# Attention with a gated feed-forward on one core: pooled PSUM banks, product streams in halves, and V products of one or two key tiles in a list-scheduled order

## The chip, the cores and the metric

The kernel runs on one core of one Trainium2 chip. The metric is the device time in microseconds of one execution; a time is the median of the runs. A core has TensorE (PE in the profile) with its weight loads (PEld), VectorE (DVE), ScalarE (ACT), GpSimd (POOL) and SyncE (SP), whose queue issues the DMAs. Each engine works through its own instructions in their order, and semaphores hold an instruction until what it needs has been done.

## The reference

```python
xn = _layernorm(x)                                   # S = 2048, D = 512
q, k, v = split((xn @ wqkv), 32 heads of 16)
p = softmax(q @ k.T * 16 ** -0.5)                    # 2048 x 2048 for each head
s = concat(p @ v) @ wo
h = (xn @ w_gate) * (xn @ w_up)                      # F = 1792
y = h @ w_down
out = x + s * silu(y)
```

All is float32 to the caller. Inside, each operand of the projections and of the feed-forward is split into a high part (float32r) and the rest, and each product is made of three terms: high x high, high x low, low x high.

## The kernel before, in words

**Units of attention.** Heads go in eight groups of four, queries in four chunks of 512: 32 units, and each unit has 16 key tiles of 128 keys, 512 rounds in all. A round has three kinds of TensorE work:

- four score products *t* (`expo`, L575): keys x queries of one head, 128 x 512, into a PSUM bank; ACT reads it with one exponential (L577) into an SBUF tile *e*, of which there are 12.
- four products *s* (`score`, L550): queries x keys, the same scores the other way round, 21 rounds ahead, from which DVE takes the row maxima (L552). The maxima of a unit are gathered (`maxima`), sent through DRAM and put as extra rows into the unit's query tile, so that *t* comes out with the maximum subtracted.
- one *turn* of V products (`pv`, L586): for each head, V of the key tile (with a column of ones for the sum) x *e*, four heads on four column groups of the array, added up over the 16 rounds in one bank. Each shows as two rows per head in the profile, because its operands are float32.

A head's *t* and *s* have a depth of 48 or 50, so they fill half of the array's rows: heads 0 and 2 the lower half, 1 and 3 the upper. Two matmuls on different halves run side by side. I call such a step of PE a slot.

**The other products.** The projections of the later heads (p), the feed-forward's gate and up products (g, u), its down products (y) and the output products (z) are worked in between, in their own order. Each has 12 terms or more per output, each cut into a lower and an upper half of the depth. `pair` (L231) makes two outputs at once: in its first half the lower terms of one run beside the upper terms of the other (L243, L247), then the halves change; ACT *looks* at one element in between (L251), so that the second half of an output waits for the first. The generator `ffn` goes over four token chunks, in each over three thirds of the 14 feature tiles: g and u of a tile, then h = u * g on DVE (L348, from PSUM and ACT's copy of g, L346), the split of h (ACT cast L306, POOL subtraction L307), and behind each third the four y outputs. POOL also splits the weights that SP loads (`split_raw`, L138 and L141, two buffers each).

**What sets the order.** A loop over the 512 rounds, written out by hand: *t* and *s* one after the other with the half changing, after the second *t* a share of the products (`Filler.part`, a number of slots given by `spread`), and at the round's end the turn of V of the round before. Small steps on DVE and ACT are put a few steps later (`soon`). PSUM's eight banks are dealt out by kind (`BUFS`): two for *t*, three for *s*, one for V, two for the products. PE, ACT and DVE take their instructions in the order of the program; POOL's and SP's are placed by the compiler's own scheduler.

**The end.** When the heads of a chunk are finished, its attention output is loaded, split by POOL (`o_split`) and multiplied with wo (z). Of the last chunk all terms but the last four heads' are made ahead (`open_pair`), and `final` adds those; `end` multiplies with silu(y), adds x and stores.

Of the kernel before, what the change touches and what calls it, by code (L numbers as in the profile page):

```python
# [19 lines left out]
P = 128  # L20
# [12 lines left out]
FFN_ROUNDS = 484  # L33
SLOTS = 24 * (NC * (NG // 2 - 1) + 1) + 36 * NF * NC
SPLIT_ROUNDS = 4
EBUFS = 12
HBUFS = 2
FINAL_AT = 8
# [8 lines left out]
def body(ctx, tc, x, wqkv, wo, wg, wu, wd, out):  # L47
# [48 lines left out]

    steps, waiting = [0], []

    def soon(n, fn):

        if n:
            waiting.append((steps[0] + n, fn))
            waiting.sort(key=lambda w: w[0])
        else:
            fn()

    def flush():
        while waiting:
            waiting.pop(0)[1]()

    def step():
        steps[0] += 1
        while waiting and waiting[0][0] <= steps[0]:
            waiting.pop(0)[1]()

# [114 lines left out]
    def pair(outs, banks, sums, more=((), ()), stop=True):  # L230

        for k in range(2):
            low, high = [*more[k], *sums[k]], sums[1 - k]
            yield k, len(low)
            if k == 0:
                outs += [psum(tag, name) for tag, name in banks]
            for n in range(len(low)):  # L240
                m = n - len(low) + len(high)
                l, r = low[n]
                nc.tensor.matmul(outs[k], l[LOWER], r[LOWER], start=k == 0 and n == 0,  # L243
                                      stop=(stop or k == 0) and n == len(low) - 1, skip_group_check=k == 1)
                if m >= 0:
                    l, r = high[m]
                    nc.tensor.matmul(outs[1 - k], l[UPPER], r[UPPER], start=k == 0 and m == 0,  # L247
                                          stop=(stop or k == 0) and m == len(high) - 1, skip_group_check=k == 1)
                yield 1
            if k == 0:  # L250
                nc.scalar.activation(look, outs[1][0:1, 0:1], AF.Copy)  # L251


# [16 lines left out]

    def proj_pair(m, which):

        outs = []
# [6 lines left out]
        for o, (_, w, c) in zip(raws, which):  # L280
            hl = qp.tile([P, 2, D], F32R, name="hl", bufs=HBUFS)
            split_rows(o, hl[:, 0], hl[:, 1])
            qk_store(hl, m, w, c)
# [143 lines left out]
    def ending():  # L427
# [70 lines left out]
        while "t" not in fst:  # L498
            yield
# [338 lines left out]
```

## Time and profile before

| | |
|---|---|
| median of 3 runs | 1816.97 us (1816.04 to 1818.2) |
| profiled execution, first to last instruction | 1815.7 us |
| mean granted TensorE clock | 0.995 |
| busy: PE, PEld | 1794.1, 991.1 us |
| busy: DVE, ACT, POOL | 1474.4, 1238.3, 580.7 us |
| DMA traffic | 145.72 MB, 80 GB/s |

The profiled execution has no time of its own beside this span; the median lies 1.3 us above it. A row of the lines view has the line, the engine, the operation, output <- inputs, partitions x elements and the count, then the busy time and the mean of one in ns, and behind the second bar the idle time of the engine just before such instructions with what ended it. A row of the timeline has the start and the length in us, the engine and the line; equal rows that follow each other are merged (x8). Matmuls overlap, so the pitch from start to start tells their cost, not their length.

### The profile page before, as it was taken

Reading aid. Unit: us, or ns where it says so; the run is one execution under the profiler, and the core shown is the slowest. Engines: PE = TensorE matmul, PEld = TensorE weight load, DVE = VectorE, ACT = ScalarE, POOL = GpSimd, SP = SyncE. Lnnn points to the kernel's source line nnn. Section 1 sums busy time; section 2 is a strip of 40 time slices with the busy share of each in tenths; the row PEclk is TensorE's granted clock in tenths of the full one; section 3 lists DMA queues with packets and bytes.
Section 4 is the critical chain, followed back from the end, with each engine's and each line's share of the span. In section 5 each row is a group of like instructions: output and inputs, shape, how many; then the busy total and the mean of one; then the engine's idle time right before and its main releaser. Section 6 shows DMA issues by size and latency. Waiting matters only on the chain.

```text
span 1815.7 us, 34194 instructions
## 1 busy us (share of the span) xinstructions
PE 1794.1 (99%) x13568; PEld 991.1 (55%) x13568; DVE 1474.4 (81%) x2456; ACT 1238.3 (68%) x2365; POOL 580.7 (32%) x647
## 2 busy tenths in 40 slices
PE   8899999999999999999999999999999999999998
PEld 5565555555555555555555555555555555555555
DVE  8488888888888888888888888888888888888832
ACT  5137676777776767777777777776767767767674
POOL 5321332431331325232132441431315323223441
PEclk9899999999999999999999999999999999999999
DMA  5424633520222122321115220411125111111352
GB/s 198 112 54 163 225 118 115 148 62 22 68 64 54 49 86 80 80 55 42 39 42 131 69 63 22 94 52 33 52 79 126 46 40 57 34 48 45 110 156 79
DMA packets 117227, 145.72 MB, mean 80 GB/s; under 512 B 12620, under 2 KB 74060, under 8 KB 114380
## 3 DMA queue, kind: packets, MB, share of 16 engines
q1 hardware_dynamic: 117068, 143.55, 27.7%
q8 instruction: 106, 1.74, 0.4%
q14 instruction: 53, 0.43, 0.1%
HBM read 95.94 MB, written 47.45 MB: 79 GB/s over the span
## 4 chain that ended last, share of the span: by engine, by line
PE 94%; DVE 2%; DMA 2%; POOL 1%; issue 0%; ACT 0%; SPq 0%; POOLq 0%; ACTq 0%; DVEq 0%
PE pv L586 27%; PE t L575 21%; PE s L550 11%; PE y L243 6%; PE u L243 5%; PE g L243 4%; PE u L247 4%; PE g L247 4%; PE y L247 3%; PE p L243 3%; PE v L224 2%; PE p L247 2%; PE z L243 1%; PE z L247 1%; DMA wdr<-in_wd_dram 1%; PE p L224 0%
## 5 line engine op out<-in xcount | busy, mean ns | idle before, releaser
L552 DVE TENSOR_REDUCE mx<-s 128x1 f32<-128x512 f32 x2048 | 1311.7, 683 | 268.5 <-PE s L550 162.7
L577 ACT ACTIVATE e<-t 128x512 f32<-128x512 f32 x2048 | 1111.9, 596 | 427.0 <-PE s L550 236.3
L550 PE MATMUL s<-ks,qs 48*128 48x512 f32 x2048 | 700.1, 427 | 10.0 <-DMA ks<-KD 8.8
L575 PE MATMUL t<-qs,ks 50*128 50x512 f32 x2048 | 705.2, 426 | 0.3 <-ACT e L577 0.3
L575 PEld LDWEIGHTS t<-qs,ks 50*128 50x128 f32 x2048 | 347.2, 185 | 499.4 <-ACT e L577 474.0
L586 PE MATMUL pv<-e,V 128*32 128x512 f32 x4096 | 545.7, 605 | 0.0
L550 PEld LDWEIGHTS s<-ks,qs 48*128 48x128 f32 x2048 | 337.4, 185 | 33.9 <-issue 12.9
L138 POOL CAST w0h<-w0r 128x512 fp32r<-128x512 f32 x60 | 36.7, 612 | 407.2 <-PE u L243 257.9
L586 PEld LDWEIGHTS pv<-e,V 128*32 128x32 f32 x4096 | 81.0, 108 | 156.5 <-issue 147.3
L352 POOL CAST dh<-wdr 128x512 fp32r<-128x512 f32 x56 | 33.8, 614 | 182.9 <-PE y L247 92.4
L247 PE MATMUL u<-fh,w0h 64*128 64x512 f32 x224 | 88.2, 394 | 0.1
L247 PE MATMUL y<-dh,hh 64*128 64x512 f32 x224 | 88.1, 393 | 0.0
L243 PE MATMUL u<-fh,w0l 64*128 64x512 f32 x224 | 88.0, 393 | 0.0
L243 PE MATMUL g<-fh,w1l 64*128 64x512 f32 x224 | 87.8, 392 | 0.0
L247 PE MATMUL g<-fl,w1h 64*128 64x512 f32 x224 | 87.8, 392 | 0.0
L243 PE MATMUL u<-fh,w0h 64*128 64x512 f32 x224 | 87.7, 392 | 0.0
L247 PE MATMUL g<-fh,w1h 64*128 64x512 f32 x224 | 87.7, 392 | 0.0
L243 PE MATMUL g<-fh,w1h 64*128 64x512 f32 x224 | 87.7, 391 | 0.0
L243 PE MATMUL u<-fl,w0h 64*128 64x512 f32 x224 | 87.6, 391 | 0.0
L243 PE MATMUL g<-fl,w1h 64*128 64x512 f32 x224 | 87.6, 391 | 0.0
L243 PE MATMUL y<-dh,hh 64*128 64x512 f32 x224 | 87.6, 391 | 0.0
L243 PE MATMUL y<-dl,hh 64*128 64x512 f32 x224 | 87.5, 391 | 0.0
(250 smaller groups left out, 2885.1 us busy)
## 6 DMA issues: line engine op xcount, KB each, us to landing
w1r<-in_wg_dram SPq DMA_DIRECT2D x56, 256.0 KB
w0r<-in_wu_dram SPq DMA_DIRECT2D x56, 256.0 KB
wdr<-in_wd_dram SPq DMA_DIRECT2D x56, 256.0 KB
qs<-QD SPq DMA_DIRECT2D x64, 192.0 KB
ks<-KD SPq DMA_DIRECT2D x12, 768.0 KB
KD<-hl SPq DMA_DIRECT2D x16, 512.0 KB
QD<-hl SPq DMA_DIRECT2D x16, 512.0 KB
OD<-tr SPq DMA_DIRECT2D x31, 256.0 KB
```

Of the source, the lines that this page charges most:

```text
L138: cast = nc.gpsimd.tensor_copy(hi, raw)
L224: nc.tensor.matmul(o, l(d), r(d), start=k == d == 0, stop=k == 2 and d == ND - 1)
L243: nc.tensor.matmul(outs[k], l[LOWER], r[LOWER], start=k == 0 and n == 0, stop=(stop or k == 0) and n == len(low) - 1, skip_group_check=k == 1)
L247: nc.tensor.matmul(outs[1 - k], l[UPPER], r[UPPER], start=k == 0 and m == 0, stop=(stop or k == 0) and m == len(high) - 1, skip_group_chec ...
L352: nc.gpsimd.tensor_copy(dh[:, i], raw)
L550: nc.tensor.matmul(o, QS[i][b:b + KB, pr, t * P:(t + 1) * P], k[b:b + KB, pr, kc * 512:(kc + 1) * 512], start=True, stop=True)
L552: nc.vector.tensor_reduce(MX[i][:, j, t, kc:kc + 1], o, axis=AX.X, op=OP.max)
L575: nc.tensor.matmul(o, k[b:b + KR, pr, kt * P:(kt + 1) * P], QS[i][b:b + KR, pr], start=True, stop=True)
L577: nc.scalar.activation(e, o, AF.Exp, scale=DH ** -0.5)
L586: nc.tensor.matmul(fst["pv"][32 * j:32 * j + 32], V[:, kt, h0:h0 + 32], es[j], start=kt == 0, stop=kt == NT - 1)
```

## The change

**Banks.** `BUFS` goes. Seven banks form one pool for *t*, *s* and all products, the eighth stays with V.

**Streams.** `pair` goes. Each output is an object `Out`: the lower halves of its terms run as one stream, then ACT looks at it, then the upper halves run in a second stream beside the lower halves of the next output. Up to two, and towards the end of one three, outputs are held.

**The order.** A class `Order` keeps a clock for PE, ACT and DVE from a table of durations (`SLOT`, `TURN`, `EXP_STEP` and others), and at each step picks what PE does: a *t* beside an *s*, one of them beside a product, two products, one alone, or a turn. Small steps are tasks with a time from which they may run.

**Turns.** A turn takes one key tile, or two where the *e* of two rounds are there; PE's order has 180 of two and 152 of one.

**Steps that change engine.** h = u * g: ACT copies u as well (L667) and POOL multiplies the two copies in SBUF (L668); DVE no longer takes part, and h has two buffers. ACT also copies both projections of what was a pair (L563, DVE had one), and makes all first y additions (L710, DVE had half). Each output has a look, 202 instead of 101.

The core of the diff:

```diff
-BUFS = {"st": 2, "s": 3, "pv": 1, "misc": 2}
+POOL = 7
+SLOT, ENTER, TURN, LEAVE, AGAIN = .229, .105, .857, .10, .105
+COPY, HIDDEN, PRODUCT, LOOK, LOOK_SEEN, RECIP = .60, .63, .68, .16, .15, .30
+RELEASE, BY_POOL, IDLE, LATE, SPLIT_WAIT, SILU_GAP = .15, 3.0, .1, 3.0, 12.0, 12.0
...
-    def pair(outs, banks, sums, more=((), ()), stop=True):
...
+    class Out:
+        def product(self, x):
+            n, ts = self.at[x], self.terms[x]
+            rows = (LOWER, UPPER)[x]
+            l, r = ts[n]
+            last = n == len(ts) - 1
+            nc.tensor.matmul(self.o, l[rows], r[rows], start=x == 0 and n == 0,
+                             stop=last and (x == 0 or not self.kept), skip_group_check=x == 1)
+            self.at[x] += 1
+            return last
+    class Order:
...
+        def turn(self, ks):
+            for n in ks:
+                pv(n // 16, n % 16, self.es.pop(n))
+                del self.eready[n]
...
+            batch = 2 if self.turns % 16 < 15 and sum(self.done) / 2 < PACE * self.turns + PACE0 else 1
...
-                    g = fp.tile([P, 512], F32, name="g", bufs=1)
-                    nc.scalar.activation(g, outs[0], AF.Copy)
-                    h = fp.tile([P, 512], F32, name="h", bufs=1)
-                    soon(1, lambda h=h, u=outs[1], g=g: nc.vector.tensor_tensor(h, u, g, op=OP.mult))
-                    soon(4, lambda h=h, hi=hh[:, i], lo=hl[:, i]: hidden(h, hi, lo))
...
+                def product():
+                    h = fp.tile([P, 512], F32, name="h", bufs=2)
+                    nc.scalar.activation(h, o.o, AF.Copy)
+                    nc.gpsimd.tensor_tensor(h, h, gs[n], op=OP.mult)
+                    hs.append(h)
+                    used.add(n)
...
+                    order_.task("act", t + BY_POOL, HIDDEN, split_hidden, gate=lambda: T.opened)
```

How the rows stand. First PE, in the feed-forward, before: the end of a round's products (y), *t* and *s*, the turn of V of one tile, and the next round.

```order
L243 MATMUL y_2_3_8894<-dh,hh 128x512
L247 MATMUL y_2_2_8893<-dh,hh 128x512
L243 MATMUL y_2_3_8894<-dl,hh 128x512
L247 MATMUL y_2_2_8893<-dl,hh 128x512
L575 MATMUL t_8_2_9038<-qs,ks_132 128x512
L550 MATMUL s_13_3_9042<-ks_132,qs 128x512
L575 MATMUL t_8_3_9045<-qs,ks_132 128x512
L550 MATMUL s_13_2_9049<-ks_132,qs 128x512
L586 MATMUL pv_8752<-e,V 32x512 x4
L575 MATMUL t_9_0_9056<-qs,ks_132 128x512
L550 MATMUL s_14_1_9060<-ks_132,qs 128x512
L575 MATMUL t_9_1_9063<-qs,ks_132 128x512
```

Now the same engine in the feed-forward of the changed kernel: every output is a bank *b*, L288 is a product term (here of y), L970 a *t*, L942 an *s*, L981 a V product.

```order
L288 MATMUL b_7046<-fh,w0l 128x512
L288 MATMUL b_7150<-dl,hh 128x512
L970 MATMUL b_7259<-qs,ks_776 128x512
L288 MATMUL b_7150<-dh,hl 128x512
L942 MATMUL b_7264<-ks_132,qs 128x512
L981 MATMUL pv_6623<-e,V 32x512 x8
L942 MATMUL b_7279<-ks_132,qs 128x512
L970 MATMUL b_7282<-qs,ks_132 128x512
L970 MATMUL b_7286<-qs,ks_132 128x512
L942 MATMUL b_7290<-ks_132,qs 128x512
L288 MATMUL b_7293<-dh,hh 128x512
L970 MATMUL b_7295<-qs,ks_132 128x512
```

The turn holds two key tiles (x8), *t* and *s* also stand beside product terms, and the terms of two different outputs (b_7046 of u and b_7150 of y) run together.

Second ACT, around the gate product of one feature tile, before: the copy of g (L346), exponentials, the cast of h (L306).

```order
L346 ACTIVATE g<-g_1_9386 128x512
L577 ACTIVATE e<-t_3_2_9595 128x512
L577 ACTIVATE e<-t_3_3_9603 128x512
L577 ACTIVATE e<-t_4_0_9614 128x512
L577 ACTIVATE e<-t_4_1_9621 128x512
L306 ACTIVATE hh<-h 128x512
```

Now, at one of the places with the shortest distance: the copy of u (L667), three exponentials and a look, and the cast of h (L253).

```order
L972 ACTIVATE e<-b_11188 128x512
L667 ACTIVATE h<-b_11029 128x512
L972 ACTIVATE e<-b_11212 128x512
L972 ACTIVATE e<-b_11222 128x512
L972 ACTIVATE e<-b_11227 128x512
L385 ACTIVATE look<-b_11108 1x1
L253 ACTIVATE hh<-h 128x512
L972 ACTIVATE e<-b_11254 128x512
```

The cast now needs POOL's product of the tile that ACT has just copied, where before it needed DVE's. The distance from copy to cast is between 4 and 12 instructions in 47 of the 56 cases, 1 in one, and over 50 in eight, where the cast waits for the next third's buffers.

Third POOL, at the same place in the changed kernel: weight splits (L125 cast, L128 subtraction), the gate product (L668), the rest of h (L254).

```order
L125 CAST w0h<-w0r 128x512
L128 TENSOR_TENSOR w0l<-w0r,w0h 128x512
L668 TENSOR_TENSOR h<-h,g 128x512
L125 CAST w1h<-w1r 128x512
L128 TENSOR_TENSOR w1l<-w1r,w1h 128x512
L254 TENSOR_TENSOR hl<-h,hh 128x512
L125 CAST w0h<-w0r 128x512
L128 TENSOR_TENSOR w0l<-w0r,w0h 128x512
```

In 45 of the 56 cases the gate product stands right behind a weight split, as here.

More of the change, by code (lines that the diff above doesn't have):

```diff
@@ L433, in big, with first @@
             return fp.tile([P, 5, 512], F32R, name=n)
[L435 to L448 removed]
+        def first():
+            fst["side"] = [big(n).bitcast(F32) for n in ("hh", "dl")]
+            fst["big", 1] = big("hl"), big("dh")
```

839 lines of the change are left out of this document (551 added, 288 removed).

## The prediction

> **What bounds the kernel now.** I read the page first: the busy line, then the chain of work that ended last.
>
> ```profile
> span 1815.7 us, 34194 instructions
> PE 1794.1 (99%) x13568; PEld 991.1 (55%) x13568; DVE 1474.4 (81%) x2456; ACT 1238.3 (68%) x2365; POOL 580.7 (32%) x647
> PE 94%; DVE 2%; DMA 2%; POOL 1%; issue 0%; ACT 0%; SPq 0%; POOLq 0%; ACTq 0%; DVEq 0%
> PE pv L586 27%; PE t L575 21%; PE s L550 11%; PE y L243 6%; PE u L243 5%; PE g L243 4%; PE u L247 4%; PE g L247 4%; PE y L247 3%; PE p L243 3%; PE v L224 2%; PE p L247 2%; PE z L243 1%; PE z L247 1%; DMA wdr<-in_wd_dram 1%; PE p L224 0%
> ```
>
> TensorE carries 94% of the chain. A busy PE may still hide pauses, since a matmul's row lasts longer than the pause to the next one, so I read the pitch, start to start, from PE's timeline of one round in the FFN (columns: start, length, engine, line, operation, tiles, shape).
>
> ```profile
> 703.37 1.06 PE L586 MATMUL pv<-e,V 128*32 128x512 f32 x8
> 704.37 0.50 PE L575 MATMUL t<-qs,ks 50*128 50x512 f32 x1
> 704.37 0.72 PE L550 MATMUL s<-ks,qs 48*128 48x512 f32 x2
> 704.71 0.39 PE L575 MATMUL t<-qs,ks 50*128 50x512 f32 x1
> 704.93 0.40 PE L243 MATMUL u<-fh,w0l 64*128 64x512 f32 x1
> ...
> 705.64 0.39 PE L243 MATMUL u<-fh,w0l 64*128 64x512 f32 x1
> ...
> 706.11 0.43 PE L550 MATMUL s<-ks,qs 48*128 48x512 f32 x1
> 706.46 1.06 PE L586 MATMUL pv<-e,V 128*32 128x512 f32 x8
> 707.53 0.50 PE L575 MATMUL t<-qs,ks 50*128 50x512 f32 x1
> ...
> 708.02 0.50 PE L575 MATMUL t<-qs,ks 50*128 50x512 f32 x1
> ```
>
> A pair of matmuls, one on each half of the rows, I call a slot. From 704.71 to 706.11 there are six steps: 0.233 us a slot. A turn of V products (four heads, two passes: 8 rows) is dearer than its own work: 1.00 from its start to the next slot (703.37 to 704.37), then 0.34 instead of 0.233 for the first slot after it, and 0.35 instead of 0.233 for the last slot before it (706.11 to 706.46). So a turn of one key tile adds 1.00 + 0.107 + 0.117 = 1.22 us to the flow of slots. The last rows show a wait: 0.49 from 707.53 to 708.02 where 0.34 was due, 0.15 lost.
>
> The order of the program before has, between its first turn and its last, 510 turns of one tile and 4482 slots. The timeline gives the two ends, and the last turn, the only one there with two tiles.
>
> ```profile
> 122.28 1.06 PE L586 MATMUL pv<-e,V 128*32 128x512 f32 x8
> 1798.46 2.25 PE L586 MATMUL pv<-e,V 128*32 128x512 f32 x16
> 1798.91 0.61 PE L586 MATMUL pv<-e,V 128*32 128x512 f32 x4
> 1799.34 0.61 PE L586 MATMUL pv<-e,V 128*32 128x512 f32 x3
> ```
>
> 1798.46 − 122.28 = 1676.2 us. 4482 x 0.233 = 1044.3 and 510 x 1.22 = 622.2 make 1666.5. Waits of PE are therefore only 1676.2 − 1666.5 = 9.7 us in all: what can still be had is in the 622 us of turns, hardly in the waits. With 0.229 a slot the same sum leaves 27.6 us of waits; that is the spread of this reading.
>
> **Turns of two tiles.** Passes inside a turn follow at 0.43 (1798.91 to 1799.34), so a second tile adds two passes, 0.86, and a turn of two adds 2.08 where two turns add 2.44: 0.36 saved each. The changed order has, from its first turn to its last, 152 turns of one tile and 179 of two ahead of a last one of two. That is 152 x 1.22 + 179 x 2.08 = 185.4 + 372.3 = 557.7 us: 64.5 less than 622.2.
>
> **Rolling streams.** Each product output now runs its lower half and later its upper half as a stream of its own, and the order puts whatever is ready beside it. It leaves 207 slots between the turns with one half empty, where before has 6. So the same matmuls take 4567 slots: 4567 x 0.233 = 1064.1, 19.8 more than before. What a half-empty slot costs is shown at the end of before, where one half runs alone:
>
> ```profile
> 1804.33 0.39 PE L243 MATMUL z<-fl,w0h 64*128 64x512 f32 x1
> 1804.56 0.39 PE L243 MATMUL z<-fh,w0l 64*128 64x512 f32 x1
> 1804.80 0.39 PE L243 MATMUL z<-fh,w1h 64*128 64x512 f32 x1
> ...
> L243 PEld LDWEIGHTS u<-fh,w0h 64*128 64x128 f32 x224 | 41.7, 186 | 6.0
> ```
>
> The pitch is 0.23 to 0.24, that of a full slot: the weight load, 186 ns in the last row (of the lines view), adds nothing. Against this stands a rule of the Trainium skill, "TensorE: Matmul & The Clock Gate", section "The mechanism": weight loads overlap a running matmul only when their row group differs. By that rule each lone half would also pay its load; the three rows show no such cost, and the case is priced as a rival below.
>
> **Head and tail.** Ahead of the first turn the changed order has 58 slots for 62: −0.9 us. Behind the last it has 48 for 24 (the output products of the last chunks, some of them lone halves): +24 x 0.233 = +5.6. Up to 3 us of these may lie beside the last heads' transposes on DVE; I take all 5.6, since PE has work on both sides of them before, too.
>
> **Sum without waits.** Between the turns 1064.1 + 557.7 = 1621.8 for 1676.2, −54.4; with −0.9 and +5.6 the span is 1815.7 − 49.7 = 1766.0.
>
> **Waits that go, and those that may come.** Before, t has two PSUM banks and s three; now all kinds draw on seven, and t may have four outstanding. So waits for ACT to free a bank should go. The engines behind are not the next bound. The lines view groups their work:
>
> ```profile
> L552 DVE TENSOR_REDUCE mx<-s 128x1 f32<-128x512 f32 x2048 | 1311.7, 683 | 268.5 <-PE s L550 162.7 <-PE t L575 85.0
> L348 DVE TENSOR_TENSOR h<-u,g 128x512 f32<-128x512 f32 x56 | 38.1, 681 | 1.0 <-POOL hl L307 0.9
> L279 DVE COPY qr<-p 128x512 f32<-128x512 f32 x13 | 8.9, 688 | 0.0
> L369 DVE COPY y<-y 128x512 f32<-128x512 f32 x8 | 5.5, 690 | 0.8
> L346 ACT ACTIVATE g<-g 128x512 f32<-128x512 f32 x56 | 33.5, 598 | 19.9 <-PE u L243 9.8 <-PE g L247 7.4
> L251 ACT ACTIVATE look<-u 1x1 f32<-1x1 f32 x56 | 9.0, 160 | 15.5 <-PE u L247 12.6
> L138 POOL CAST w0h<-w0r 128x512 fp32r<-128x512 f32 x60 | 36.7, 612 | 407.2 <-PE u L243 257.9 <-PE g L247 102.6 <-PE p L243 23.5
> L141 POOL TENSOR_TENSOR w0l<-w0r,w0h 128x512 fp32r<-128x512 f32 x60 | 77.5, 1291 | 0.2
> L314 POOL TENSOR_TENSOR y<-e,y 128x512 f32<-128x512 f32 x16 | 21.7, 1357 | 1.1
> 122.30:1800.00 1677.70, 1676.80 (x13055) 913.52 (x13054) 1383.37 (x2277) 1195.43 (x2290) 531.60 (x586) 1.00 0.27 76
> ```
>
> The last row is the windows view of the same stretch: PE, weight loads, DVE 1383, ACT 1195, POOL 532 us, then the granted clock of 1.00. DVE loses the gate products, the copies of half the projections and of half the first y: 38.1 + 8.9 + 5.5 = 52.5, and is at 1331 of 1622 us, 82%. ACT gains 56 copies of u (33.5 by the row of g), 21 of the others (13 projections, 8 first y: 12.6) and 101 looks (the order has 202 for 101, at 0.16: 16.2): 1257 of 1622, 78%. POOL gains 56 products at 1.36 as in L314's row: 76, to 608. All three keep idle time, so each of these edits costs nothing while its queue is not waited for.
>
> One queue is new on the path: ACT copies u, POOL multiplies, ACT casts h (L253), and behind that cast stand the exponentials. In 45 of 56 cases POOL splits a weight tile just ahead of the product, and that split is released by the same u matmul: 0.61 + 1.29 + 1.36 = 3.26 us after it. ACT reaches the cast after its copy and, by the order, a median of 9 further instructions. Four exponentials in a row took 2.29 us (0.57 each), and the first of two began 0.44 after its matmul:
>
> ```profile
> 702.78 0.40 PE L575 MATMUL t<-qs,ks 50*128 50x512 f32 x1
> 703.22 1.08 ACT L577 ACTIVATE e<-t 128x512 f32<-128x512 f32 x2 [0.33 <-PE s L550]
> 706.87 2.29 ACT L577 ACTIVATE e<-t 128x512 f32<-128x512 f32 x4
> 701.80 1.09 ACT L577 ACTIVATE e<-t 128x512 f32<-128x512 f32 x2 [0.61 <-PE t L575]
> ```
>
> So ACT comes to the cast at 0.44 + 0.60 + 9 x 0.57 = 6.2 us after that matmul, 2.9 later than POOL is done; with 4 instructions between (the least but one; four cases have 4 or fewer) at 3.3, just in time. Weights are still loaded ahead by SP, whose queue holds the same transfers. I price the change's waits from both sides: nothing, or, where half of the 56 casts were 1.9 late (one split), 53. I take 8, near the 9.7 of before, because the median slack is larger than a split.
>
> Forecast of the span: 1766.0 + 8 = 1774. The median of the three runs of before, 1817.0, lies 1.3 above the profiled span, so 1775 us.
>
> **The rivals.**
> Best case: the order leaves no waits, and slots are 0.229. Then 1045.8 + 557.7 = 1603.5 between the turns, −72.7, and 4.6 more outside: 1747.6, with 1.3 for the median 1749; at 0.233 it is 1767. For it: seven banks. Against it: transfers, POOL and the heads' small steps stay outside any fixed order. Chance 0.22.
> POOL late: the 53 us above, wholly or by half, give 1767 + 27 to 1767 + 53: 1794 to 1820. For it: POOL's idle before L138 is long only because it stands at its queue's head waiting for PE, and the h product now stands in that queue. Against it: the slack of 2.9. It decides from 0.8 us per product. Chance 0.15: 0.11 of it still faster, 0.03 the same, 0.01 slower.
> No change: a lone half pays its weight load too, 0.186. 201 more lone halves make 37, on 1775 that is 1812. The three rows at 1804 speak against it: 0.02, counted as "same". (It is what the Trainium skill's page on TensorE, named above, would have.)
> Slower: the turn of two starves the next. ACT already stands idle 0.61 after a turn of one (701.80); a turn of two keeps PE from making t for 0.86 longer, and the es of the following turn come late by as much as ACT has no stock. At 0.5 of the 0.86 lost in each of 179 it is 90 us: 1865; above 0.26 per turn the 46 us between 1767 and 1813 are gone. Against it: t may wait in four of the seven banks, and 12 e tiles less the 8 of the turn leave 4 to fill, 4 x 0.57 = 2.3 us of work for ACT, longer than the turn's 1.00 + 0.86. Chance 0.08.
>
> **How the numbers follow.** Forecast 0.53 (1760 to 1793), best case 0.22, POOL late 0.15, lone halves dear 0.02, starved turns 0.08. A measurement of this kernel tells about 0.2%, 3.6 us, from no change. Faster: 0.53 + 0.22 + 0.11 = 0.86. Same: 0.02 + 0.03 = 0.05. Slower: 0.08 + 0.01 = 0.09. The range leaves out the lower third of the best case, the starved turns and the worst of POOL late, some 0.2 together: 1755 to 1810.
>
> **What would show it.** After: some 332 turns in PE's timeline, with x16 rows of about 1.92; 0.23 between slots, lone halves too; DVE near 1420 and POOL near 655 us on the page; waits of PE's loads for ACT no larger per turn. Wrong would be: ACT's cast of h idle for POOL by tens of us, t or pv loads waiting for e by 0.3 or more after turns of two, or lone halves at 0.4.

## The result and the profile after

The changed kernel takes **1841.6 us** (median of 4 runs, 1837.5 to 1847.6) against 1817.3 for the kernel before, measured beside it: ratio 1.0137, 95% interval 1.0117 to 1.0157. It is slower; I had forecast 1775.

The page of the profiled execution (1847.6 us) answers the lines shown of before: span, busy times, the chain by engine.

```profile
span 1845.8 us, 34982 instructions
PE 1796.2 (97%) x13568; PEld 1061.4 (58%) x13568; DVE 1400.6 (76%) x2377; ACT 1259.5 (68%) x2543; POOL 658.8 (36%) x705
PE 90%; DMA 4%; DVE 3%; POOL 2%; issue 1%; ACT 1%; SPq 0%; POOLq 0%; ACTq 0%
```

TensorE's share of the chain falls from 94% to 90%, and DMA's rises from 2% to 4%. DVE and POOL are busy for about what I had worked out (1420 and 655). So the work is as planned and the time is not: look next at the stretch between the first and the last turn of V. First its ends, from PE's timeline, then the waits of PE in it (total, times, longest).

```profile
121.53 1.06 PE L981 MATMUL pv<-e,V 128*32 128x512 f32 x8
1822.07 1.92 PE L981 MATMUL pv<-e,V 128*32 128x512 f32 x16
```

```profile
PE b L970 <- DMA qs<-MD: 14.6, 5, 5.9
PE b L288 <- ACT look L385: 5.8, 1, 5.8
PE b L288 <- POOL hl L254: 5.1, 3, 4.1
```

The stretch takes 1822.07 - 121.53 = 1700.5 us where the sum without waits had 1621.9. The **excess** is 78.7 us, against 9.7 before; I use this number below for every kernel (stretch, less 0.233 a slot, 1.22 a turn of one, 2.08 a turn of two, with that kernel's own counts). Only some 28 us of it (25.5 in these rows, the rest in small ones) are waits of TensorE for another engine or a transfer; the first row, 14.6 us in 5 waits, is a unit's first key tile waiting for its maxima.

What follows a wait is seen in the windows view (us, then PE, PEld, DVE, ACT, POOL busy, granted clock, DMA share, GB/s) and in the chain at one of the five, where the queue's rows (SPq) and the transfer lead to the *t* at 981.93.

```profile
353.00:359.00 6.00, 4.79 (x19) 2.09 (x21) 1.38 (x2) 3.80 (x8) 5.35 (x6) 0.50 0.47 145
985.00:989.00 4.00, 4.00 (x25) 1.27 (x23) 1.61 (x3) 1.15 (x2) 0.00 (x0) 0.70 0.50 72
1100.00:1120.00 20.00, 20.00 (x158) 10.46 (x157) 17.05 (x28) 15.55 (x32) 7.56 (x7) 1.00 0.17 51
```

```profile
973.78 0.32 SPq L63
...
974.19 0.26 SPq L60
...
974.50 7.30 DMA qs<-MD
...
981.93 0.76 PE b L970
982.69 0.46 PE b L288 x3
983.15 0.39 PE b L942
983.55 0.03 PE b L970
983.58 0.39 PE b L288
```

An undisturbed stretch (1100 to 1120) has a clock of 1.00. Around the first of the two waits it is 0.50, behind the second 0.70 (half speed ends there at 987.4), and from 983.15 to 983.55 a slot takes 0.40 where 0.233 was due. The records of the granted clock show 44.4 us at half speed in the stretch, in blocks of 3.4 us or twice that, all but two next to a wait in which TensorE is idle for 1.3 us or more (the two, at 1704 and 1752, lie where the products run short: 20 matmul rows stand in the 4 us from 1700, and 36 in the 4 us from 1100); before has none between its first and its last turn. The Trainium skill states the mechanism ("TensorE: Matmul & The Clock Gate", section "HAM oscillation — how this bites in real kernels"): TensorE's clock falls to half after an idle gap of more than about 3.4 us. The trace agrees on the half and on the block of 3.4, but here idle gaps of 1.3, 1.8 and 2.4 us (at 767, 491 and 604) were enough.

From turn to turn the excess divides so: 49.0 us in the 15 pieces that hold some half clock, of which some 24 are the waits themselves and 25 the slow slots beside them; 11.5 in pieces that lose more than 0.3 us without it; some 18 spread over 300 pieces at less than 0.3 each.

### The profile page after: what moved, and what is told of

It reads as the page before. It is cut to its first block, busy times and chain, and to the rows that moved or that the text cites. A ratio compares the mean times of both kernels' runs of the same rounds, so it can differ in the third digit from the quotient of the medians.

```text
span 1845.8 us, 34982 instructions
## 1 busy us (share of the span) xinstructions
PE 1796.2 (97%) x13568; PEld 1061.4 (58%) x13568; DVE 1400.6 (76%) x2377; ACT 1259.5 (68%) x2543; POOL 658.8 (36%) x705
## 3 DMA queue, kind: packets, MB, share of 16 engines
q1 hardware_dynamic: 117068, 143.55, 27.3%
## 4 chain that ended last, share of the span: by engine, by line
PE 90%; DMA 4%; DVE 3%; POOL 2%; issue 1%; ACT 1%; SPq 0%; POOLq 0%; ACTq 0%
PE b L288 32%; PE pv L981 26%; PE b L970 15%; PE b L942 14%; PE v L211 2%; DVE mx L944 1%; DMA qs<-MD 1%; DMA MD<-mt 1%; PE s L942 1%; DVE st L150 0%; DMA ks<-KD 0%; PE p L211 0%; POOL xl L186 0%; ACT e L972 0%; DMA wdr<-in_wd_dram 0%
## 5 line engine op out<-in xcount | busy, mean ns | idle before, releaser
L944 DVE TENSOR_REDUCE mx<-b 128x1 f32<-128x512 f32 x1964 | 1229.6, 683 | 328.3 <-PE b L942 141.4
L972 ACT ACTIVATE e<-b 128x512 f32<-128x512 f32 x2048 | 1103.1, 600 | 455.8 <-PE b L970 225.0
L970 PE MATMUL b<-qs,ks 50*128 50x512 f32 x2048 | 780.8, 420 | 16.0 <-DMA qs<-MD 14.6
L942 PE MATMUL b<-ks,qs 48*128 48x512 f32 x1964 | 757.6, 423 | 0.7 <-DVE mx L944 0.3
L981 PE MATMUL pv<-e,V 128*32 128x512 f32 x4096 | 516.0, 608 | 0.0
L970 PEld LDWEIGHTS b<-qs,ks 50*128 50x128 f32 x2048 | 368.2, 186 | 179.7 <-issue 48.1
L942 PEld LDWEIGHTS b<-ks,qs 48*128 48x128 f32 x1964 | 341.4, 186 | 194.6 <-ACT e L972 62.7
L981 PEld LDWEIGHTS pv<-e,V 128*32 128x32 f32 x4096 | 99.9, 109 | 222.5 <-issue 212.4
L288 PE MATMUL b<-fh,w0h 64*128 64x512 f32 x500 | 200.7, 403 | 6.0 <-ACT look L385 5.8
L288 PE MATMUL b<-fh,w1h 64*128 64x512 f32 x504 | 201.5, 403 | 0.3 <-ACT look L385 0.3
L288 PE MATMUL b<-fh,w1l 64*128 64x512 f32 x504 | 198.2, 398 | 0.0
L288 PE MATMUL b<-fl,w1h 64*128 64x512 f32 x504 | 198.0, 396 | 0.0
L288 PE MATMUL b<-fl,w0h 64*128 64x512 f32 x500 | 197.0, 397 | 0.0
L288 PE MATMUL b<-fh,w0l 64*128 64x512 f32 x500 | 196.6, 398 | 0.0
L288 PE MATMUL b<-dh,hh 64*128 64x512 f32 x448 | 161.6, 407 | 0.6 <-ACT hh L253 0.5
L288 PE MATMUL b<-dh,hl 64*128 64x512 f32 x448 | 154.0, 400 | 5.1 <-POOL hl L254 5.1
L288 PE MATMUL b<-dl,hh 64*128 64x512 f32 x448 | 156.9, 398 | 0.0
L288 PEld LDWEIGHTS b<-fh,w0h 64*128 64x128 f32 x500 | 93.4, 187 | 20.2 <-ACT look L385 7.9
L288 PEld LDWEIGHTS b<-fh,w1h 64*128 64x128 f32 x504 | 93.6, 187 | 19.2 <-issue 4.6
L288 PEld LDWEIGHTS b<-fh,w1l 64*128 64x128 f32 x504 | 93.7, 187 | 8.5 <-issue 2.5
L288 PEld LDWEIGHTS b<-fl,w1h 64*128 64x128 f32 x504 | 93.7, 187 | 7.6 <-issue 1.7
L288 PEld LDWEIGHTS b<-fl,w0h 64*128 64x128 f32 x500 | 93.2, 187 | 7.8 <-issue 2.0
```

Source lines behind the costliest of these rows:

```text
L288: nc.tensor.matmul(self.o, l[rows], r[rows], start=x == 0 and n == 0, stop=last and (x == 0 or not self.kept), skip_group_check=x == 1)
L942: nc.tensor.matmul(o, QS[i][b:b + KB, pr, t * P:(t + 1) * P], k[b:b + KB, pr, kc * 512:(kc + 1) * 512], start=True, stop=True)
L944: nc.vector.tensor_reduce(MX[i][:, j, t, kc:kc + 1], o, axis=AX.X, op=OP.max)
L970: nc.tensor.matmul(o, k[b:b + KR, pr, kt * P:(kt + 1) * P], QS[i][b:b + KR, pr], start=True, stop=True)
L972: nc.scalar.activation(e, o, AF.Exp, scale=DH ** -0.5)
L981: nc.tensor.matmul(fst["pv"][32 * j:32 * j + 32], V[:, kt, h0:h0 + 32], es[j], start=kt == 0, stop=kt == NT - 1)
```

## The experiments

Sixteen kernels. "Counts" is the span by my sum without waits; "maxima" is PE's wait for the maxima's transfer (us, times); "half" is time at half clock between the first and the last turn.

| kernel | us | ratio, interval | counts | excess | maxima | half |
|---|---|---|---|---|---|---|
| before | 1817.3 | 1 | 1806.0 | 9.7 | 0 | 0 |
| changed | 1841.6 | 1.0137 (1.0117-1.0157) | 1766.1 | 78.7 | 14.6, 5 | 44.4 |
| 1 maxima on ScalarE's queue | 1850.9 | 1.0183 (1.0168-1.0198) | 1772.9 | 76.1 | 24.5, 6 | 37.5 |
| 2 product on VectorE | 1838.7 | 1.0113 (1.0097-1.0128) | 1772.6 | 64.7 | 10.0, 6 | 30.7 |
| 3 before, turns of two | 1979.7 | 1.0895 (1.0877-1.0913) | 1714 | 264 | 0 | 0 |
| 4 list waits 12 us for maxima | 1885.3 | 1.0374 (1.0357-1.0391) | 1792 | 87.4 | 2.9, 3 | 68 |
| 5 keys held | 1825.9 | 1.0059 (1.0044-1.0074) | 1766.1 | 60.2 | 7.1, 3 | 27.3 |
| 6 = 1 + 5 | 1818.0 | 1.0008 (0.9999-1.0018) | 1772.9 | 45.6 | 0 | 10.2 |
| 7 = 1 + 2 + 5 | 1827.0 | 1.0067 (1.005-1.0084) | 1775.3 | 51.0 | 0.5, 1 | 13.7 |
| 8 before, late maxima | 1886.3 | 1.039 (1.0374-1.0405) | 1806.0 | 80.0 | 52.6, 9 | 61.4 |
| 9 = 5, weights by POOL | 1858.5 | 1.0229 (1.0215-1.0243) | 1766.1 | 89.5 | 12.2, 2 | 41.0 |
| 10 = 9, splits 18 us | 1863.4 | 1.0256 (1.0242-1.027) | 1767.6 | 92.8 | 12.4, 2 | 54.6 |
| 11 = 6, third buffer, 18 us | 1820.4 | 1.0017 (1.0009-1.0026) | 1772.5 | 45.6 | 0 | 6.8 |
| 12 = 5, third buffer, 18 us | 1820.9 | 1.002 (1.0011-1.003) | 1767.6 | 50.5 | 3.7, 2 | 13.7 |
| 13 = 12, slot 0.239 | 1828.2 | 1.006 (1.0048-1.0072) | 1760.1 | 67.9 | 7.9, 3 | 30.7 |
| 14 = 11, slot 0.239 | 1825.0 | 1.0047 (1.0031-1.0063) | 1762.3 | 66.1 | 0 | 30.7 |
| 15 changed, slot 0.239 | 1837.1 | 1.0101 (1.0087-1.0116) | 1759.2 | 76.7 | 8.2, 3 | 41.0 |
| 16 = 12, slot 0.248 | 1840.9 | 1.0126 (1.0111-1.0142) | 1740.7 | 98.2 | 3.4, 3 | 20.5 |

**The queue of the maxima.** The first theory was that the maxima's transfers stand behind loads of weights in SyncE's queue. Its rivals were POOL being late, and turns of two that starve.

Kernel 1 issues those transfers on ScalarE's queue, as tasks of the list:

```diff
-    dma(MD[i]...., mt)                      # in rest(), on SyncE's queue
-    dma(QS[i][row:row + 2]...., md[e])
+    self.task("act", t + .3, .5, lambda: to_dram(si), urgent=True, then=...)
+    self.task("act", t + 3.0, .55, lambda: from_dram(si), urgent=True, then=...)
```

> The changed kernel, but the store of a unit's maxima and their two loads into the query tile are issued by ACT's queue, as small tasks of the list, not by SP's. Counted in its order, PE's work without waits is 6.8 us more than in the changed kernel (165 turns of two for 180). Queue theory (the maxima stand behind weight and key loads in SP's queue and among their packets; PE waits, and its clock then falls to half for some us): the five waits of t for the maxima (17 us) and the half-speed stretches behind them (24 us, 12 lost) go: 1842 - 29 + 7 = about 1820, and no t waits 1 us or more for the maxima. Starvation theory (turns of two leave ACT and DVE without stock, and the pooled banks couple them): nothing of that goes: 1842 to 1850.

It came out slower still, at 1850.9, with six waits for the maxima where five had been. This is the chain at one of them:

```profile
975.35 0.23 ACTq L977
...
975.62 8.53 DMA qs<-MD
```

```profile
974.63 0.32 SPq L63 DMA_DIRECT2D ks<-KD  x1
...
976.11 0.43 SPq L63 DMA_DIRECT2D ks<-KD  x1
```

On a queue of its own the transfer of 8 KB still takes 8.53 us, and it runs beside two loads of the next keys, 768 KB each (second fence: SyncE's queue). All six waits stand at every fourth unit, where the heads' group changes and those loads leave. So the queue alone is not the cause. The Trainium skill says the same of queues in general ("DMA: Bandwidth & Descriptors", section "Issuing engines are not separate DMA queues"): whichever engine starts them, transfers share the same DMA engines. These rows agree.

Kernel 2 takes the gate product back to VectorE, which reads the bank and one SBUF tile (the list then lets the cast follow 0.3 us behind it, not 3.0):

```diff
-                    nc.scalar.activation(h, o.o, AF.Copy)
-                    nc.gpsimd.tensor_tensor(h, h, gs[n], op=OP.mult)
+                    nc.vector.tensor_tensor(h, o.o, gs[n], op=OP.mult)
```

> The changed kernel, but the gate product is again made by DVE from PSUM and ACT's copy of g; ACT's copy of u and POOL's product are gone. PE's work without waits is 6.5 us more by its order. If POOL's product behind the weight splits were the main loss (my rival of a late POOL): about 50 us less, 1795. Queue theory: only the one wait behind POOL's splits and the h product near 354 us goes (7 us and the slow clock after it), and DVE takes 38 us more in its idle time: 1835 to 1845. Starvation theory: 1842 to 1855.

It gains 2.9 us on the changed kernel: its counts are 6.5 higher and its excess 14.0 lower. Six waits for the maxima stay, so POOL's product is not where most of the 79 us are.

Kernel 3 puts turns of two into the hand-written order of before, and nothing else:

```diff
+            if kt % 2 == 0 and len(prev) == 2:
+                for p in prev:
+                    pv(*p)
...
+            prev.append((i, kt, es))
```

> The kernel before, with one edit: the turns of V for two key tiles are done together, every second round; banks, products and small steps as before. Counted: 256 turns of two for 510 of one, 4474 slots between the turns; PE's work without waits is 92 us less. Queue theory (turns of two cost what the rows say; the loss lies in the queues): 1817 - 92 plus waits for two t banks during the longer turn, at most 0.2 in each of 256: 1725 to 1775. Starvation theory (each turn of two costs the next one 0.3 us or more): 1800 or above.

It takes 1979.7 us. The timeline shows why, at the end of a round that has no turn, six slots and more behind a turn of two:

```profile
702.32 0.67 PE L575 MATMUL t<-qs,ks 50*128 50x512 f32 x2
702.55 0.44 PE L550 MATMUL s<-ks,qs 48*128 48x512 f32 x1
703.40 0.50 PE L575 MATMUL t<-qs,ks 50*128 50x512 f32 x1 [0.40 <-ACT e L577]
...
703.89 0.50 PE L575 MATMUL t<-qs,ks 50*128 50x512 f32 x1
```

The last two *t* of the round (702.32 and 702.55) are followed at once by the first two of the next one. With two banks, *t* waits for ScalarE to empty them: 0.85 from 702.55 to 703.40 and 0.49 from there to 703.89, where 0.233 a slot was due. The excess of 264 us is about 1.04 for each of 254 turns of two. So a price like that of the starvation that I gave 0.08 exists in the old order, but not by the way that I named: no turn waits for its *e*; four *t* in a row wait for two banks. In the changed kernel it is gone: away from half clock, a turn of two has 0.09 of excess and a turn of one 0.10. Whether the list or the seven banks remove it was not separated.

Kernel 4 only tells the list that the maxima are known 12 us after the transpose, not 6:

```diff
-MAXIMA, MAXIMA_WAIT, REST, KNOWN = .45, 4.0, .15, 6.0
+MAXIMA, MAXIMA_WAIT, REST, KNOWN = .45, 4.0, .15, 12.0
```

> The changed kernel with one constant changed: the list takes the maxima as there 12 us after their last step on DVE instead of 6, so it lets t of the next unit begin later and puts products there. Counted: 146 turns of two for 180, 327 lone halves for 207; PE's work without waits is 26 us more. Queue theory: four of the five waits of t for the maxima (all but the longest, 6.3 us) and their slow clock go, about -25: 1840 to 1845. Starvation theory: they do not matter, +26 less some turns of two: 1860 to 1870.

The waits for the maxima nearly go, but the time is worse: the list now waits itself, spends its products doing so (counts 1792, 327 lone halves for 207), and has none left at the end, where 19 pieces with half clock stand.

**What stands beside and ahead of the transfers.** The theory now: the maxima's small transfers run beside the key loads, or stand behind weight loads, and each late first key tile costs its wait and the half clock. Kernels 5, 6 and 8 keep the order on TensorE of the kernel that they are made from, matmul for matmul.

Kernel 5 is the changed kernel with one edit: the key loads wait for an exponential some 16 us into a unit.

```diff
-        if kt == 0 and g + 1 < NG and c == 1:
+        if kt == 0 and g == 0 and c == 1:
             load_k(g + 1)
...
+        if (c, kt, j) == (0, 4, 3) and 0 < g < NG - 1:
+            load_k(g + 1, after=at.ins.name)      # at: the exponential just issued
```

> The changed kernel, with the order of TensorE, ScalarE and VectorE as it was, word for word; only the loads of the next heads' keys (two of 768 KB every fourth unit, which leave as soon as their buffer is free, and that is when the next unit's maxima are due) are made to wait for the exponentials of key tile 4 of the group's first unit, some 16 us later. Theory (the excess of 78.7 us is waits of a unit's first key tile for its maxima, each with a stretch of half clock behind it): the waits at 767.4 and 981.9, which stand beside key loads, go with their half clock, 3.1 + 9.3 us by the turn-to-turn sums, and the three beside the loads of weights (491, 604, 1617) stay: 1828 to 1833. If the maxima were late for another reason (the transpose that goes in late, or the queue alone), or if the clock falls by itself: 1838 to 1845, with the half clock still there.

It measures 1825.9. PE's row of waits for the maxima falls from 14.6 in 5 to this:

```profile
PE b L971 <- DMA qs<-MD: 7.1, 3, 3.2
```

The waits at 767 and 982 are gone with their half clock (3.1 and 9.3 us by the turn-to-turn sums), and those beside weight loads stay (482, 592 and 1594). The one at 354, where ScalarE and POOL were late, falls as well, from 5.8 us to 1.1: POOL's splits there had waited for loads of down weights, 3.2 us at 346.7, and key loads had left at 322.6 and 332.7; now they leave at 345.4 and 346.0. Moving the key loads is worth 15.7 us in all.

Kernel 6 holds the keys in kernel 1.

> The kernel with the maxima's transfers on ScalarE's queue, its order word for word, and the key loads held back as in the run beside this one. There six waits at the groups' boundaries were left, 40.2 us with their half clock of 76.1 in all. Theory (key loads slow the 8 KB transfers down): all six go, no half clock is left between the first and the last V product, 1850.9 - 40 = 1811 (1805 to 1818), faster than the kernel before by a little. If the rows of key loads and late maxima only coincide: 1845 to 1852.

It measures 1818.0, 32.9 us less than kernel 1 with the same matmuls in the same order. Between 400 and 1600 us PE's largest waits are these two:

```profile
PE b L288 <- POOL hl L254: 1.3, 3, 0.6
PE b L983 <- ACT e L985: 0.5, 2, 0.3
```

Not one is for the maxima (a third of 0.2 us is for VectorE). Against the changed kernel that is 23.6 us less, nearly the 24.3 lost against before. But the kernel is now as fast as before, not 40 us faster: the excess falls from 78.7, and 45.6 us of it stay.

Kernel 7 adds kernel 2's edit.

> The same with the gate product back on VectorE. Its counts give 1775.3 without waits (1772.9 with the product on POOL). If what is left is the small excess (about 20 us in parts under 0.3 us) and the end's waits (8 to 15 us): 1803 to 1812, about the same as the run beside it; the wait of 6.2 us at 354, which came through POOL, is gone. If POOL was what made the rest late: under 1800. If the product on VectorE makes the maxima's steps later: over 1815 with waits of the first key tile.

At 1827.0 it is 9 us slower than kernel 6. The wait at 338 through POOL is gone, but single waits of 1 to 2 us come back near 1600 and 1660, with half clock, and it lands in the range that I had given to a late VectorE. I had expected no difference; here POOL is the better place for the product.

Kernel 8 measures the price of a wait by itself, in the kernel before: the maxima make their trip more often than once.

```diff
+            for _ in range({1: 2, 3: 3}.get(i % 4, 1)):
                 dma(MD[i].rearrange("f (b q) -> b f q", b=4), mt)
...
```

> The kernel before, its order word for word, but in every second unit the maxima make the trip through the memory twice (units 1, 5, 9 ...) or three times (3, 7, 11 ...), so that the first key tile waits: by the rows, a trip takes some 5 to 6 us, of which 2 to 4 us were spare, so 8 waits of 1 to 4 us and 8 of 6 to 10 us, some 60 to 100 us in all, which the trace gives. Theory (a wait of TensorE of 2 us or more takes the clock with it): behind the waits stands half clock, of 3.4 us behind the short ones and 6.8 us or more behind the long ones, so that the time goes up by the waits plus 25 to 60 us. If the half clock of the changed kernel came from its turns of two or its pace, and not from the waits: the time goes up by the waits alone, and the clock's mean stays at 0.99 or above.

The first row is its waits of PE. Then come the windows of one wait (269.6 to 279) and of what follows, and the timeline at that place.

```profile
PE t L576 <- DMA qs<-MD: 52.6, 9, 9.0
```

```profile
269.60:279.00 9.40, 0.62 (x8) 0.00 (x0) 0.72 (x2) 0.48 (x1) 0.00 (x0) 0.70 0.22 52
279.00:283.50 4.50, 4.43 (x20) 2.89 (x24) 2.33 (x4) 2.16 (x4) 0.00 (x0) 0.50 0.00 0
283.50:290.00 6.50, 6.50 (x56) 3.58 (x52) 5.48 (x11) 4.05 (x9) 3.36 (x4) 1.00 0.22 84
```

```profile
279.07 0.76 PE L576 MATMUL t<-qs,ks 50*128 50x512 f32 x1 [8.84 <-DMA qs<-MD]
...
280.06 0.62 PE L243 MATMUL p<-fl,w0h 64*128 64x512 f32 x1
...
280.48 0.62 PE L243 MATMUL p<-fh,w0l 64*128 64x512 f32 x1
```

The clock falls during the wait and is still 0.50 for 4.5 us after it; a slot takes 0.42 (280.06 to 280.48). No other part of the change is in this kernel, so waits alone bring the half clock. Its price is smaller than I had expected: the time rises by 69.8, of which 52.6 are the nine waits, and the rest, 17 us, is about 2 us for each wait. Two trips in place of one make TensorE wait in one unit of eight (2.9 us at 607), so before has some 5 us to spare ahead of a unit's first key tile.

**What is left.** Kernel 9 is kernel 5 with the loads of the down and output weights and of the head rows on POOL's queue, kernel 10 also changes an estimate in the list.

```diff
-            dma(raw, wd[f * P:(f + 1) * P])
+            nc.gpsimd.dma_start(raw, wd[f * P:(f + 1) * P])
...
-RELEASE, BY_POOL, IDLE, LATE, SPLIT_WAIT, SILU_GAP = .15, 3.0, .1, 3.0, 12.0, 12.0
+RELEASE, BY_POOL, IDLE, LATE, SPLIT_WAIT, SILU_GAP = .15, 3.0, .1, 3.0, 18.0, 12.0
```

> The changed kernel with the key loads held back, and the loads of the down and output weights and of the heads' rows (the tiles named wdr, w1r and w0r in the ends) issued on POOL's queue, which splits them, not on SyncE's; TensorE, ScalarE and VectorE keep the changed kernel's order word for word. With the keys held alone it was 1825.9. Theory (the maxima's store stands behind weight loads that wait for their buffer): the waits of the first key tile at 482, 592 and 1594 go, 2.3 + 4.1 + 6.2 us with their half clock; the wait for the heads' splits near 1639 (7.2 us with its half clock) stays: 1813 (1808 to 1818). If the stores were late for another reason: 1823 to 1828. If issuing loads costs POOL enough to make its splits and products late: over 1828, with waits of products on POOL.

> The same, and the list told that the splits of a 512-token block of head rows take 18 us, not 12: the order is the same up to the last block of units, and the counts give 1767.6 without waits in place of 1766.1. If the wait of 4.6 us near 1639 is the list's estimate (the chain of loads and splits on POOL took it past 1661 where the list had 1657), it goes, 7.2 us with its half clock, and 1.5 us are paid: 1807 (1802 to 1813). If the ends of the stretch are underfed whatever the estimate: 1811 to 1818.

Both failed, at 1858.5 and 1863.4. The chain of kernel 9 at the place of the wait at 482 shows the reason:

```profile
486.68 0.62 POOL w1h L125
...
487.38 1.27 POOL w1l L128
...
488.67 0.39 SPq L60
...
489.10 2.52 DMA MD<-mt
...
491.63 0.24 SPq L60
...
491.92 1.51 DMA qs<-MD
...
493.57 0.76 PE b L971
```

POOL is later, since it now waits for its own loads, and the next load in SyncE's queue (of gate weights, SPq at 488.67) waits for POOL's split w1l, with the maxima's store again behind it. The queue's order shows again as a cause, and the cure was wrong. Without key loads beside it the small transfer takes 1.51 us, not 7.3. Kernel 10's estimate gained nothing here.

Kernels 11 and 12 give the weights' loads a third buffer, so that fewer of them block the queue, and keep the 18 us.

```diff
-            raw = fst["fp"].tile([P, D], F32, name="wdr", bufs=2)
+            raw = fst["fp"].tile([P, D], F32, name="wdr", bufs=3)
```

> The kernel with the maxima's transfers on ScalarE's queue and the keys held back (1818.0, no different from the kernel before), with a third buffer for the loads of the down weights, so that the first third's five splits stand less long ahead of the gate product on POOL (a wait of 4.8 us at 338, 6.4 to 7.2 us with its half clock), and with 18 us in place of 12 for the splits of head rows in the list; order the same up to the last units, counts 1772.5. If the wait at 338 and the one at 1677 (3.0 us) come from these: 1818 - 7 - 3 = 1808 (1804 to 1813), faster than before by 0.3 to 0.6 percent. If POOL is late there for its own work and the end is underfed anyway: 1815 to 1820.

> The changed kernel with the keys held back (1825.9), its transfers on SyncE's queue as they were, with the third buffer and the 18 us; order the same as the changed kernel's up to the last units, counts 1767.6. A third buffer lets the fourth and fifth load of a burst leave one split (some 3 us) earlier, so the maxima's store behind them does too. If the queue theory holds, the waits of the first key tile at 482 and 592 shrink or go (2.3 + 4.1 us), that at 1639 too (7.2 us, 1.5 paid), the one near 1594, which stands behind output weights, may stay: 1813 (1809 to 1820). If it fails: 1824 to 1828.

SyncE's queue at the wait near 482, first in kernel 5, then in kernel 12 (start, time until the last of the row left):

```profile
465.56 9.55 SPq L60 DMA_DIRECT2D wdr<-in_wd_dram  x5
476.70 0.38 SPq L60 DMA_DIRECT2D w1r<-in_wg_dram  x1
477.17 0.51 SPq L60 DMA_DIRECT2D MD<-mt  x1
```

```profile
466.32 8.68 SPq L60 DMA_DIRECT2D wdr<-in_wd_dram  x5
476.59 0.38 SPq L60 DMA_DIRECT2D w1r<-in_wg_dram  x1
477.06 0.53 SPq L60 DMA_DIRECT2D MD<-mt  x1
```

The maxima were transposed at 473.11 and 473.88; their store leaves 4.1 us later in kernel 5 and 3.2 later in kernel 12. The five loads take less long, but the gate weights' load (w1r), which waits for POOL, still stands ahead of the store. The wait at 482 shrinks from 2.17 us start to start to 1.10, that at 592 from 2.57 to 1.53 (the view of waits puts this one down to VectorE, so the table's 3.7 leaves it out); with what the end gains it is 5.0 us on kernel 5, not the 13 that I expected. Kernel 11 does not gain on kernel 6: its wait at 338 only shrinks (7.2 to 4.9 us with its half clock), and the end loses as much.

Kernels 13 to 16 change one number of the list, the time of a slot, from 0.229. With 0.239, about the pitch measured in the changed order, the list closes more turns of two (13: 194 of two, 124 of one); with 0.248 nearly all are (16: 242 and 28).

```diff
-SLOT, ENTER, TURN, LEAVE, AGAIN = .229, .105, .857, .10, .105
+SLOT, ENTER, TURN, LEAVE, AGAIN = .239, .105, .857, .10, .105
```

> The changed kernel with keys held, third buffer and 18 us (1820.9, 50.5 us above its counts), and the list told that a slot takes 0.239 us, as measured in this order, not 0.229. The list then closes more pairs of turns: 124 turns of one and 194 of two, 4539 slots, counts 1760.1 in place of 1767.6. If the excess stays what it is: 1813. If part of the small excess (19 us in parts under 0.3) or of the end's 17 us comes from the list's clock running ahead of TensorE: 1803 to 1810. If further turns of two starve for exponentials: 1818 and over.

> The same with the maxima's transfers on ScalarE's queue (1820.4 with the slot at 0.229; counts 1772.5, now 1762.3). By the counts alone 1810; with less of the small excess 1800 to 1808; if turns of two starve, 1818 and over. No wait of a first key tile for a transfer either way.

> The changed kernel with the slot of 0.239 alone: counts 1759.2 in place of 1766.1. If the waits of the first key tile are set by SyncE's queue and the key loads, they stay, with their half clock: 1834 (1825 to 1845). If they came from the list's clock running ahead of TensorE: under 1820.

> As the first of these, but with a slot of 0.248, which nothing measured: the list closes nearly every turn as a pair (28 of one, 242 of two, counts 1740.7). If a turn of two costs what the rows say, 2.05 us and under 0.1 us of wait: 1794 (1788 to 1800). If pairs that close that often leave the exponentials behind (the rival of my prediction, 1.04 us each in the hand-written order): 20 us and more come back, 1815 to 1840, in waits of under 1 us before the key tiles and products behind a turn.

Three of the four went the other way from their counts. 13 and 14 save 7.5 and 10.2 us by count and come out 7.3 and 4.6 slower; waits grow or come at other places (in 13, 7.9 us in 3 for the maxima, of them 3.4 at 590 and 3.9 at 1490), and half clock appears at 1306 in 13 and at 638 and 1307 in 14 with no wait of 0.9 us beside it. 15 gains 4.5 us where its counts fall by 6.9. Its time fits the theory that the waits stay, but they are not the same waits: of the five of the changed kernel only the one at 604 stands, now 4.9 us for 2.4; one of 2.6 comes at 1504, the one through ScalarE and POOL near 354 grows from 5.8 to 9.6, and those at 491, 767, 982 and 1617 are gone with no edit to the loads. At 767 the maxima's loads now leave at 759.8 and the next keys' at 762.9 and 764.4, where they left at 760.1 and at 758.8 and 761.6. So the order decides which first key tile meets which load, and the list's slot time alone does not take the loss away. In 16 the counts fall by 26.9 and the time rises by 20: away from half clock a turn of two, with the slots up to the next turn, now has 0.30 us of excess, three times that of kernel 12. A fit of the turn-to-turn times puts this into the slots, 0.247 in place of 0.239, and not into the turns (2.07 for 2.05), so it is not the loss of kernel 3. What holds the slots was not separated.

## Why the prediction was wrong

**Turns, slots and lone halves: right.** Away from disturbed pieces a fit of the turn-to-turn times gives 1.20 for a turn of one, 2.05 for a turn of two (1.22 and 2.08 used), and no extra price for a lone half. The 201 more lone halves cost their slot and nothing else; that rival falls.

**Head and tail: right.** The first turn comes at 121.53 for 122.28 (-0.75, forecast -0.9); behind the last turn's start there are 23.8 us for 17.3 (+6.5, forecast +5.6).

**The slot: slightly short.** The same fit gives 0.239 a slot. Away from turns and half clock, a product stood beside a *t* or *s* in some 20 slots before; now it does in nearly 1900, and their mean is 0.241 beside a *t* and 0.243 beside an *s*, where two products take 0.232 before and 0.234 now. At 0.009 above 0.233 that is 17 us, most of the 18 in small parts. I had taken the pitch from an order that hardly has such slots. Whether it comes from banks that are emptied a little late or from the two halves slipping against each other was not separated; kernels 13 and 14 show only that the list's own slot time does not cure it.

**The step that failed** is "I take 8, near the 9.7 of before". It measured 78.7. By the turn-to-turn sums some 25 of that are the five waits of a first key tile for its maxima with their half clock, some 15 the two waits behind POOL (354 and 1661) with theirs, some 6 the half clock at 1704 and 1752, and the rest small parts, of which the slot has most. For the largest of these waits, those for the maxima, the bound rested on "weights are still loaded ahead by SP, whose queue holds the same transfers". The transfers are the same, but not where the rest stands. In the hand-written order a unit's first *t* came 15 to 16 us after its maxima, with 5 us to spare (kernel 8). In the list the transpose of the maxima comes later (8.0 us after them in the median, 6.5 before), and the first *t* is put as early as 12.5 us after them. The queue itself was no better before: SyncE let the maxima's store leave over 1 us late in nine units there and in five now. These rows are the worst of them in the kernel before, VectorE's transpose, the load ahead of the store, the store, and the first *t*, which does not wait:

```profile
1368.79 0.20 DVE L563 STREAM_TRANSPOSE mt<-mm 128x32 f32<-128x32 f32 x1
1368.85 5.09 SPq L53 DMA_DIRECT2D wdr<-in_wd_dram  x3
1374.03 0.53 SPq L53 DMA_DIRECT2D MD<-mt  x1
1378.88 0.50 PE L575 MATMUL t<-qs,ks 50*128 50x512 f32 x1
```

From transpose to first *t* there were 9.6 us in the median; where nothing waits, the list leaves 6.9. The spare time is used up, and a load that leaves ahead or beside can now hold TensorE, as it did in five of 32 units. The best case's argument against itself ("transfers ... stay outside any fixed order") was right, and I gave it no price. I had bounded the casts behind POOL and not the first key tiles, and I had left out that TensorE slows down behind a wait.

**POOL late: in two places, not in half of the casts.** One cast of 56 waited long for POOL's product (row below), and one product of TensorE waited 4.1 us at 1661 for POOL's rest of h. Both stood in POOL's queue behind splits that waited for their loads, 3.2 us at 346.7 and 2.1 at 1659.5. With half clock the two cost some 15 us where I had 27 to 53. Taking the product away gains 2.9 us in kernel 2, at an excess 14.0 lower, and loses 9 once the transfers are in order (kernel 7).

```profile
353.48 0.63 ACT L253 ACTIVATE hh<-h 128x512 fp32r<-128x512 f32 x1 [7.59 <-POOL h L668]
```

**Turns of two that starve: not in this order.** The price per turn is 1.04 us in the hand-written order (kernel 3), where *t* waits for its banks and no turn for its *e*; it is 0.09 in the changed order, and 0.30 in slots, not turns, if the list is pushed (kernel 16). That is in line with the four outstanding *t* that I had set against it, but no run changed the banks alone.

**What stays open.** With the maxima in time, 45 us of excess remain in the best kernel (6): about 19 in small parts, 7 at one place behind POOL (338), 10 from 1626 to 1727, where the products run short, 9 in single pieces. None of the versions is faster than the kernel before; kernel 6 cannot be told from it. Loads of gate and up weights with more buffers were not tried.

## What to carry to other kernels

A term "waits, as before" needs its own bound when the order is remade: list each small transfer that TensorE's next work hangs on, its spare time before and after, and which large loads leave at the same moment. A list that places work by time treats transfers as constants; give the late ones slack by moving what collides with them (here one dependency on the key loads, 16 to 33 us), not by a longer constant, which cost 44. And price a wait of TensorE above its length: here about 2 us more each.

## What the runs showed of the hardware

A pause of TensorE does not decide on half clock by its length alone: of 78 idle times of 1.3 us or more 66 have it within or close behind, but 1.8 (kernel 5, 482) and 2.1 (kernel 2, 1344) have not, nor have 0.7 and 1.0 (kernel 12, 482 and 592), and some blocks have no long pause beside them. What all the traces share is a grid: within a run all blocks start a whole number of 3.41 us apart and last a whole number of them, and in the 3.41 us ahead of each of the 89 blocks at most 15 matmul rows start (17 once), where nine in ten of the steps at full clock have 24 to 30. Few starts are not enough for certain: 32 steps with 15 or fewer kept the full clock.

A slot at half clock takes 0.39 to 0.43 for 0.233. An 8 KB transfer landed in 1.5 us (kernel 9), and in 7.3 and 8.5 beside two loads of 768 KB, on SyncE's queue (changed kernel) and on ScalarE's (kernel 1). A matmul that had its half of the rows to itself paid nothing for its weight load of 186 ns: the pitch stayed 0.23 to 0.24, and 201 more of them cost their slots alone.
